# Output products of a fused convolution and SwiGLU kernel: the first group packed two quarters to a PSUM bank, with no filler products

## The chip, the cores and the metric

The kernel runs on one core of a Trainium2 chip. The metric is the device time of one launch in microseconds, the median of several runs. The kernel before takes 2728.72 us (three runs, 2728.63 to 2729.05).

## The reference, cut to what matters

```
# lightweight causal convolution: 7 taps per head, softmax over the taps
w = softmax(weight)                              # (8 heads, 7)
attn[b, s, h, :] = sum_k w[h, k] * x_pad[b, s + k, h, :]     # d_model 192
x = attn.reshape(32768, 192)

# RMS norm and SwiGLU, no bias
xn = x / sqrt(mean(x * x) + 1e-6) * rms_g
g, val = xn @ w_gate, xn @ w_val                 # (192, 1536) each
out = (silu(g) * val) @ w_out                    # (1536, 192), 32768 tokens
```

Everything is float32.

## The kernel before, in words

**Tiling.** The 32768 tokens are cut into 32 "pairs" of 1024 tokens; a pair is two groups (`g` = 0, 1) of 512 tokens. TensorE is used as two halves of 64 rows: the lower half (`h` = 0, partitions 0 to 63) and the upper half (`h` = 1). Each half runs a stream of its own products, and the two streams run beside each other. The eight PSUM banks of 128 x 512 float32 are split the same way: four for each half, handed out by two lists, `free[0]` and `free[1]`. A bank is taken from the head of the list when a product first needs one, and is appended when the last instruction that reads it has been emitted.

**Two stages for each pair.** In the first stage (`unit`, four times for each pair) the lower half computes the gate products and the upper half the value products. The contraction over 192 is three blocks of 64, and a unit covers three of the twelve blocks of 128 hidden columns. Instead of 18 products of 512 columns, each half does 15, on sums of the operands (`xc`, sums of tokens' blocks, and `wf`, sums of weights). Results are put together afterwards by ScalarE (A), VectorE (V) and GpSimd (G). All of it is in a written-out table, `PLAN`: each row has a time in ticks, a half, an engine and an action. `P` is a product, `F` copies a bank into another bank, onto which later products accumulate, `S` copies a bank to SBUF, `D` and `R` add a tile to a bank, `G` is the silu and `M` the product of gate and value. Products of a half stand 100 ticks apart; the upper half lags by `LAG` = 138 ticks; a unit starts every `SPAN` = 1509 ticks.

In the second stage (`outer`) the hidden tile `ht` (1536 x 1024 tokens) is multiplied by `w_out`. For each group `g` and each quarter `j` of 128 tokens there are twelve products (`f` = 0 to 11) of 192 columns in each half, 96 for a half and pair. The lower half contracts rows 0 to 63 of every block, the upper half rows 64 to 127. `low` copies the lower half's bank to `o_sb` (ScalarE), `upp` adds the upper half's bank (VectorE), and each then gives its bank back. `store` writes the group out. A product of this stage takes `STEP` = 37.5 ticks.

**What sets the order.** Everything is emitted from one heap, `line`, by planned tick, and within an engine instructions run in the order of emission; the ticks fix the order only, not the time. Engines wait for one another by semaphores, for instance a product that opens a bank waits for the last reader of that bank.

**Banks in the second stage.** For `g` = 0 the last unit's blocks (`f` = 9 to 11) are ready late, so all four quarters first do `f` = 0 to 8, each in a bank of its own (all four banks of the half), and then `f` = 9 to 11, each quarter followed by an evacuation of 192 columns. For `g` = 1 two quarters share a bank (columns 0 to 191 and 192 to 383) and are evacuated together, 384 columns at a time.

**The filler products.** [...] A bank that held two quarters has columns 384 to 511 unwritten, so the kernel issues an extra product of 128 columns into them (line 734) for the second shared bank of `g` = 1, which is the bank that the first `F` copy of the next pair takes:

```
            if g and j == 3 and f == 0:
                nc.tensor.matmul(
                    out=bank(h, bks[h])[:, 2 * D :],
                    ...
                    rhs=wo_sb[HALF[h], f, 0 : T - 2 * D], start=False, stop=True,
```

The condition holds once for each half and pair: 64 such products in all, each of which the profile shows as two passes.

**Other work beside.** The convolution of the pair after next (`conv`), its norm, its transposition through a DRAM scratch (`place`, `fetch`) and its operand sums (`x_sums`) are queued between these on ScalarE, VectorE and the DMA queue. In pair 0 the first stage is `plain` instead of `unit`: 18 plain products, emitted in the order of a string.

Lines that the steps use: the product of a unit is line 629, `F` and `S` on ScalarE are line 638 and on VectorE 640 and 642, `D` and `R` are line 651, the output product is line 723, the filler line 734, `low` line 743, `upp` line 747, `x_sums` line 565.

Of the kernel before, what the change touches and what calls it, by code (L numbers as in the profile page):

```python
# [19 lines left out]
def kernel(  # L20
# [10 lines left out]
    nc = tc.nc  # L31
    P = nc.NUM_PARTITIONS

    B, S, D = x.shape
# [8 lines left out]
    T = 512  # L43
# [7 lines left out]
    FC = DF // P  # L51
    NF = 3
# [129 lines left out]
    wo_sb = cst.tile([P, FC, D], F32, name="wo_sb")  # L182
# [28 lines left out]
    def load_out(i):  # L211
# [28 lines left out]
        out=taps[:], in0=w_sb[:], in1=stat[:].to_broadcast([P, H, K]), op=ALU.subtract  # L240
# [7 lines left out]
        out=taps[:], in0=taps[:], in1=ssum[:].to_broadcast([P, H, K]), op=ALU.mult  # L248
# [179 lines left out]
    HALF = (LOW, UPP)  # L428
# [116 lines left out]
    def x_op(i):  # L545
        return xb[:, i // KP, i % KP, :] if i < 2 * KP else xc[:, i - 2 * KP, :]
# [23 lines left out]
    free = [[0, 1, 2, 3], [0, 1, 2, 3]]  # L570

    def bank(half, i):
        return ps[half * 4 + i]


    whole = {(h, i) for h in range(2) for i in range(4)}


    line = []
# [2 lines left out]
    def put(at, do):  # L582
        heapq.heappush(line, (at, next(tick), do))
# [7 lines left out]
    def unit(u, base):  # L591


        ht = big.tile([P, 2, NF, T], F32, name="ht")
        bk, tl = {}, {}

        def hv(o):
            return ht[:, o // NF, o % NF, :]

        def new(v, h, product=False):  # L600
            bk[v, h] = free[h].pop(0)
            if product:
                whole.add((h, bk[v, h]))
            assert (h, bk[v, h]) in whole
            return bank(h, bk[v, h])[:]

        def old(v, h):
            return bank(h, bk[v, h])[:]

        def grab(k):  # L610
            tl[k] = tiles.pop(0)
            return tl[k][:]

        def tile_of(t, h):

            if (t, h) in tl:
                return tl[t, h][:]
            return hv(t[0]) if h else tl["g", t[0]][:]

        def plus(s):  # L620
            return ALU.add if s > 0 else ALU.subtract

        def do(h, eng, act, v, *rest):
            *rest, freed = rest
            e = {"V": nc.vector, "G": nc.gpsimd}.get(eng)
            if act == "P":
                i = rest[0]
                first = (v, h) not in bk
                nc.tensor.matmul(  # L629
                    out=new(v, h, True) if first else old(v, h), lhsT=wf[u][HALF[h], WAT[i], :],  # L630
                    rhs=x_op(XOP[i])[HALF[h]], start=first, stop=True, skip_group_check=True,
                )
            elif act in "FS":
                w, s = rest if act == "F" else (v, 1)
                src = old(w[0], h) if (w[0], h) in bk else tile_of(w, h)
                dst = new(v, h) if act == "F" else grab((v, h))
                if eng == "A":
                    nc.scalar.activation(out=dst, in_=src, func=AF.Copy, scale=float(s))  # L638
                elif s < 0:
                    e.tensor_scalar(out=dst, in0=src, scalar1=-1.0, scalar2=None, op0=ALU.mult)  # L640
                else:
                    e.tensor_copy(out=dst, in_=src)
            elif act == "C":
                a, b, s = rest
                a, b = tile_of(a, h), tile_of(b, h)
                e.tensor_tensor(out=grab((v, h)), in0=a, in1=b, op=plus(s))
            elif act in "DR":
                t, s = rest
                t, src = tile_of(t, h), old(v, h)
                dst = src if act == "D" else hv(v) if h else grab(("g", v))  # L650
                e.tensor_tensor(out=dst, in0=src, in1=t, op=plus(s))  # L651
            elif act == "G":
                src = tl["g", v][:] if v in results else old(v, 0)
                dst = src if v in results else grab(("g", v))
                nc.scalar.activation(out=dst, in_=src, func=AF.Silu)  # L655
            else:
                src = hv(v) if v in results else old(v, 1)
                e.tensor_tensor(out=hv(v), in0=src, in1=tl["g", v][:], op=ALU.mult)  # L658
            for k in freed:
                if k[0] == "b":  # L660
                    free[h].append(bk.pop((int(k[1]), h)))
                else:
                    tiles.append(tl.pop(("g", int(k[1])) if k[0] == "g" else (k, h)))

        for at, *a in PLAN:
            put(base + at, functools.partial(do, *a))
        return ht
# [48 lines left out]
    def outer(p, hts, base):  # L716


        def mm(h, bks, g, j, w, f, first, give=None):
            if first:  # L720
                bks[h] = free[h].pop(0)
                whole.discard((h, bks[h]))
            nc.tensor.matmul(  # L723
                out=bank(h, bks[h])[:, w : w + D],
                lhsT=hts[f // NF][HALF[h], g, f % NF, j * P : (j + 1) * P],
                rhs=wo_sb[HALF[h], f, :], start=(f == 0 and w == 0),
                stop=(f == FC - 1), skip_group_check=True,
            )

            if g and j == 3 and f == 0:
                nc.tensor.matmul(  # L734
                    out=bank(h, bks[h])[:, 2 * D :],
                    lhsT=hts[f // NF][HALF[h], g, f % NF, j * P : (j + 1) * P],
                    rhs=wo_sb[HALF[h], f, 0 : T - 2 * D], start=False, stop=True,
                    skip_group_check=True,
                )
                whole.add((h, bks[h]))  # L740

        def low(dst, bks, n):
            nc.scalar.copy(out=dst, in_=bank(0, bks[0])[:, 0:n])  # L743
            free[0].append(bks[0])

        def upp(dst, bks, n):
            nc.vector.tensor_tensor(out=dst, in0=bank(1, bks[1])[:, 0:n], in1=dst, op=ALU.add)  # L747
            free[1].append(bks[1])

        def store(g, o_sb):  # L750
            r = p * PT + g * T
            nc.sync.dma_start(
                out=out[r : r + T, :].rearrange("(j p) d -> p j d", p=P), in_=o_sb[:]
            )

        n = 0

        def mms(bks, g, j, w, fs, first):
            nonlocal n
            for i, f in enumerate(fs):  # L760
                for h in range(2):
                    at = base + n * STEP + h * LAG
                    put(at, functools.partial(mm, h, bks, g, j, w, f, first and i == 0))
                n += 1

        def evac(dst, bks, w):
            put(base + n * STEP + OVER, functools.partial(low, dst, bks, w))
            put(base + n * STEP + LAG + OVER, functools.partial(upp, dst, bks, w))

        for g in range(2):  # L770
            o_sb = outs.tile([P, T // P, D], F32, name="o_sb")
            if g == 0:

                bks = [{} for _ in range(4)]
                for j in range(4):
                    mms(bks[j], g, j, 0, range(0, FC - NF), True)
                for j in range(4):
                    mms(bks[j], g, j, 0, range(FC - NF, FC), False)
                    evac(o_sb[:, j, :], bks[j], D)
            else:  # L780
                for j in range(0, 4, 2):
                    b = {}
                    mms(b, g, j, 0, range(FC), True)
                    mms(b, g, j + 1, D, range(FC), False)
                    evac(o_sb[:, j : j + 2, :].rearrange("p j d -> p (j d)"), b, 2 * D)
            put(base + n * STEP + LAG + OVER + 1, functools.partial(store, g, o_sb))
# [33 lines left out]
    hts = []  # L820
    p, sl, v = plain(hts)
# [27 lines left out]
    for p in range(PAIRS):  # L849
        base = p * PAIR  # L850
        if p > 0:
            hts = []
            pl = place(p + 1)
            for u in range(NU):
                at = base + u * SPAN
# [51 lines left out]
```

## Time and profile before

| quantity | value |
|---|---|
| time, median of 3 | 2728.72 us |
| span of the profiled execution | 2724.8 us |
| PE busy | 2693.3 us, 99% of the span |
| VectorE, ScalarE, GpSimd busy | 84%, 81%, 46% |
| TensorE clock granted | 0.999 |
| one pair, from unit to unit (1304.28 to 1387.51) | 83.23 us |
| of it: four units | 51.81 us |
| of it: output products | 31.42 us |
| filler products in all (line 734) | 128 passes of 64x128 |

The profile counts a float32 product as two passes, each with its weight load (PEld) and its MATMUL. In a window of the timeline, the start of a MATMUL is when its turn in its half's stream came; the start of a weight load is usually the start of the MATMUL before it in the same half[...].

### The profile page before, as it was taken

What the parts mean: (1) busy time and instruction counts of PE and PEld (TensorE: products, weight loads), DVE (VectorE), ACT (ScalarE), POOL (GpSimd) and SP (SyncE); (2) the same over time, 40 slices, a digit from 0 to 9 for tenths busy, and PEclk for the clock granted to TensorE, in tenths of its full rate; (3) what the DMA queues carried; (4) which work ended last, traced back from release to release, by engine and by line L of the source; (5) the groups of instructions that cost most, each with busy time, mean ns of one, the idle gap of its engine ahead of it and who ended that gap; (6) DMA issues with size and microseconds to landing.
All of it is one profiled execution on the core that took longest, in us unless ns stands there. A gap on an engine that the chain in (4) does not pass through costs nothing.

```text
span 2724.8 us, 54269 instructions
## 1 busy us (share of the span) xinstructions
PE 2693.3 (99%) x20202; PEld 2071.0 (76%) x20202; DVE 2286.5 (84%) x3654; ACT 2212.3 (81%) x5026; POOL 1242.6 (46%) x1029
## 2 busy tenths in 40 slices
PE   6999999999999999999999999999999999999999
PEld 4767888777888778877777777778777777766777
DVE  8888888888889888888888888888898888888854
ACT  7788888888888888888888888888888888888854
POOL 3854344454344543444543445434445443454333
PEclk9999999999999999999999999999999999999999
DMA  5211222121222112121112221122211122211110
GB/s 145 82 42 44 67 57 68 42 52 54 56 68 62 41 45 67 57 68 43 51 54 56 68 62 42 45 67 57 68 44 52 52 56 68 62 42 44 48 36 13
DMA packets 94584, 152.90 MB, mean 56 GB/s; under 512 B 6768, under 2 KB 64880, under 8 KB 90232
## 3 DMA queue, kind: packets, MB, share of 16 engines
q1 hardware_dynamic: 93760, 149.41, 21.1%
q8 instruction: 158, 2.59, 0.4%
q14 instruction: 106, 0.87, 0.1%
q10 hardware_dynamic: 560, 0.03, 0.0%
HBM read 99.87 MB, written 49.55 MB: 55 GB/s over the span
## 4 chain that ended last, share of the span: by engine, by line
PE 96%; DVE 2%; DMA 1%; POOL 0%; ACT 0%; issue 0%; SPq 0%; DVEq 0%; POOLq 0%; ACTq 0%
PE ps L629 59%; PE ps L723 36%; PE ps L683 1%; DVE y L384 0%; DMA xb<-xd 0%; DMA x_sb<-in_x_dram 0%; POOL wf L321 0%; DVE xc L565 0%; PE ps L734 0%; DVE y L368 0%; ACT m L378 0%; DVE ht L700 0%; ACT xb L515 0%; DVE wf L291 0%; PE ps L495 0%
## 5 line engine op out<-in xcount | busy, mean ns | idle before, releaser
L629 PE MATMUL ps<-xc,wf 64*128 64x512 f32 x4960 | 1522.7, 593 | 2.6 <-DVE xc L565 2.6
L629 PEld LDWEIGHTS ps<-xc,wf 64*128 64x128 f32 x4960 | 771.2, 187 | 392.6 <-issue 209.8
L723 PE MATMUL ps<-wo_sb,ht 64*128 64x192 f32 x12288 | 1052.4, 323 | 2.0 <-DVE o_sb L747 1.8
L723 PEld LDWEIGHTS ps<-wo_sb,ht 64*128 64x128 f32 x12288 | 1047.7, 187 | 4.8 <-DVE o_sb L747 2.1
L629 PE MATMUL ps<-xb,wf 64*128 64x512 f32 x2480 | 1020.3, 589 | 0.0
L658 POOL TENSOR_TENSOR ht<-ht,tls 128x512 f32<-128x512 f32 x414 | 520.5, 1275 | 358.2 <-ACT tls L655 357.6
L638 ACT ACTIVATE tile<-ps 128x512 f32<-128x512 f32 x825 | 484.0, 596 | 139.9 <-PE ps L629 126.8
L629 PEld LDWEIGHTS ps<-xb,wf 64*128 64x128 f32 x2480 | 435.4, 187 | 199.0 <-issue 115.5
L378 ACT ACTIVATE m<-x_sb,taps 128x192 f32<-128x192 f32 x1520 | 543.4, 443 | 5.7 <-DMA x_sb<-in_x_dram 5.0
L384 DVE TENSOR_TENSOR y<-y,m 128x1536 f32<-128x1536 f32 x190 | 335.0, 1763 | 83.8 <-ACT m L378 78.8
L638 ACT ACTIVATE tls<-ps 128x512 f32<-128x512 f32 x663 | 376.0, 599 | 27.6 <-PE ps L629 16.1
L658 POOL TENSOR_TENSOR ht<-ht,tile 128x512 f32<-128x512 f32 x206 | 260.7, 1274 | 175.2 <-ACT tile L655 174.9
L401 POOL TENSOR_SCALAR r<-ss 128x8 f32<-128x8 f32 x31 | 27.2, 879 | 640.0 <-ACT sq L395 639.9
L655 ACT ACTIVATE tls<-tls 128x512 f32<-128x512 f32 x414 | 254.9, 625 | 16.5 <-DVE tls L651 15.0
L638 ACT ACTIVATE ps<-ps 128x512 f32<-128x512 f32 x372 | 216.3, 581 | 46.5 <-PE ps L629 35.7
L651 DVE TENSOR_TENSOR ht<-ps,tls 128x512 f32<-128x512 f32 x331 | 220.8, 681 | 0.0
L747 DVE TENSOR_TENSOR o_sb<-ps,o_sb 128x192 f32<-128x192 f32 (+1 forms) x192 | 77.5, 419 | 150.6 <-PE ps L629 107.8
L651 DVE TENSOR_TENSOR ht<-ps,tile 128x512 f32<-128x512 f32 x289 | 192.3, 681 | 0.0
L651 DVE TENSOR_TENSOR ps<-ps,tls 128x512 f32<-128x512 f32 x166 | 116.2, 700 | 87.8 <-PE ps L629 84.7
L651 DVE TENSOR_TENSOR tls<-ps,tile 128x512 f32<-128x512 f32 x248 | 166.9, 682 | 0.2 <-PE ps L629 0.2
L640 DVE TENSOR_SCALAR ps<-ps 128x512 f32<-128x512 f32 x248 | 164.1, 695 | 0.0
L743 ACT COPY o_sb<-ps 128x192 f32<-128x192 f32 (+1 forms) x192 | 70.3, 366 | 96.5 <-PE ps L723 96.5
(103 smaller groups left out, 2242.6 us busy)
## 6 DMA issues: line engine op xcount, KB each, us to landing
xb<-xd SPq DMA_DIRECT2D x124, 384.0 KB, 6.2
x_sb<-in_x_dram SPq DMA_DIRECT2D x24, 1344.0 KB, 5.8
out_dram<-o_sb SPq DMA_DIRECT2D x64, 384.0 KB, 2.6
xd<-nt SPq DMA_DIRECT2D x124, 192.0 KB, 3.4
x_sb<-in_x_dram SPq DMA_DIRECT2D x8, 1176.0 KB, 8.0
ht<-in_moe_w_gate_dram SPq DMA_DIRECT2D x12, 192.0 KB, 8.2
ht<-in_moe_w_val_dram SPq DMA_DIRECT2D x12, 192.0 KB, 6.4
tls<-in_moe_w_out_dram SPq DMA_DIRECT2D x8, 192.0 KB, 6.3
```

The source lines that it names most:

```text
L378: nc.scalar.mul(m[:, :, hs], xk[:, :, hs], taps[:, h, k : k + 1])
L384: nc.vector.tensor_tensor(out=y[:], in0=y[:], in1=m[:], op=ALU.add)
L629: nc.tensor.matmul(out=new(v, h, True) if first else old(v, h), lhsT=wf[u][HALF[h], WAT[i], :], rhs=x_op(XOP[i])[HALF[h]], start=first, st ...
L638: nc.scalar.activation(out=dst, in_=src, func=AF.Copy, scale=float(s))
L640: e.tensor_scalar(out=dst, in0=src, scalar1=-1.0, scalar2=None, op0=ALU.mult)
L651: e.tensor_tensor(out=dst, in0=src, in1=t, op=plus(s))
L655: nc.scalar.activation(out=dst, in_=src, func=AF.Silu)
L658: e.tensor_tensor(out=hv(v), in0=src, in1=tl["g", v][:], op=ALU.mult)
L683: nc.tensor.matmul(out=bank(h, bks[h])[:], lhsT=wf[u][HALF[h], k * NF + f, :], rhs=xb[HALF[h], g, k, :], start=(k == 0), stop=(k == KP - 1 ...
L723: nc.tensor.matmul(out=bank(h, bks[h])[:, w : w + D], lhsT=hts[f // NF][HALF[h], g, f % NF, j * P : (j + 1) * P], rhs=wo_sb[HALF[h], f, :] ...
L743: nc.scalar.copy(out=dst, in_=bank(0, bks[0])[:, 0:n])
L747: nc.vector.tensor_tensor(out=dst, in0=bank(1, bks[1])[:, 0:n], in1=dst, op=ALU.add)
```

## The change

The first group packs two quarters to a bank, as the second group did already. In `g` = 0, quarters 0 and 1 share one bank, quarters 2 and 3 another; they are evacuated 384 columns at a time, after the second quarter's last product. In `g` = 1, quarters 0 and 1 take the oldest free bank, and quarters 2 and 3 take one that has already been used so in this pair ("used"). So three banks of a half are partly written in a pair and the fourth stays whole. The filler products are gone. In the units, `pick` chooses by kind: an `F` copy takes the first free bank that is whole, a first product prefers one that is not, and makes it whole.

```diff
+    def pick(h, full):
+        i = next((i for i in free[h] if ((h, i) in whole) == full), free[h][0])
+        free[h].remove(i)
+        return i
...
         def new(v, h, product=False):
-            bk[v, h] = free[h].pop(0)
+            bk[v, h] = pick(h, not product)
...
         def mm(h, bks, g, j, w, f, first, give=None):
             if first:
-                bks[h] = free[h].pop(0)
+                bks[h] = free[h].pop(0) if first is True else pick(h, False)
                 whole.discard((h, bks[h]))
...
-            if g and j == 3 and f == 0:
-                nc.tensor.matmul(
-                    out=bank(h, bks[h])[:, 2 * D :],
-                    lhsT=hts[f // NF][HALF[h], g, f % NF, j * P : (j + 1) * P],
-                    rhs=wo_sb[HALF[h], f, 0 : T - 2 * D], start=False, stop=True,
-                    skip_group_check=True,
-                )
-                whole.add((h, bks[h]))
...
             if g == 0:
-                bks = [{} for _ in range(4)]
+                bks = [{}, {}]
                 for j in range(4):
-                    mms(bks[j], g, j, 0, range(0, FC - NF), True)
+                    mms(bks[j // 2], g, j, j % 2 * D, range(0, FC - NF), j % 2 == 0)
                 for j in range(4):
-                    mms(bks[j], g, j, 0, range(FC - NF, FC), False)
-                    evac(o_sb[:, j, :], bks[j], D)
+                    mms(bks[j // 2], g, j, j % 2 * D, range(FC - NF, FC), False)
+                    if j % 2:
+                        dst = o_sb[:, j - 1 : j + 1, :].rearrange("p j d -> p (j d)")
+                        evac(dst, bks[j // 2], 2 * D)
             else:
                 for j in range(0, 4, 2):
                     b = {}
-                    mms(b, g, j, 0, range(FC), True)
+                    mms(b, g, j, 0, range(FC), "used" if j else True)
                     mms(b, g, j + 1, D, range(FC), False)
```

More of the change, by code (lines that the diff above doesn't have):

```diff
@@ L762, in mms @@
                     at = base + n * STEP + h * LAG
-                    put(at, functools.partial(mm, h, bks, g, j, w, f, first and i == 0))
+                    put(at, functools.partial(mm, h, bks, g, j, w, f, first if i == 0 else False))
                 n += 1
```

## The prediction

> **What bounds the kernel now.** I read the page's busy times and groups first, then the chain of waits over two pairs, then the two stages of one pair, then single instructions around the places where the change moves a bank.
>
> ```profile
> PE 2693.3 (99%) x20202; PEld 2071.0 (76%) x20202; DVE 2286.5 (84%) x3654; ACT 2212.3 (81%) x5026; POOL 1242.6 (46%) x1029
> ...
> L734 PE MATMUL ps<-wo_sb,ht 64*128 64x128 f32 x128 | 24.4, 270 | 0.0
> ```
>
> ```profile
> 1305.65 50.75 PE ps L629 x235
> ...
> 1357.22 26.73 PE ps L723 x327
> 1383.95 0.03 PE ps L734
> 1383.98 1.22 PE ps L723 x14
> 1385.19 0.11 PE ps L734
> 1385.31 2.44 PE ps L723 x30
> ...
> 1388.88 50.75 PE ps L629 x235
> ```
>
> ```profile
> 1304.28:1356.08 51.81, 51.81 (x248) 32.30 (x247) 45.37 (x75) 44.72 (x83) 31.26 (x25) 1.00 0.09 24
> 1356.08:1387.51 31.42, 31.42 (x386) 31.42 (x384) 25.55 (x39) 24.72 (x76) 6.06 (x5) 1.00 0.40 108
> ```
>
> The second block is the chain of waits: between pairs it never leaves PE. The third is one pair's two stages (span, then PE, PEld, DVE, ACT, POOL): PE is busy in all of both. The pairs repeat every 83.23 us, so whatever shortens the PE stream of a pair by t, without a new wait, shortens the kernel by about 31 t (pair 0 is different, below).
>
> [...] passes of one half start 0.162, about 0.11 and 0.429 us apart. [...] here a load starts 0.43 us before the MATMUL that uses it in the 512-column stage. [...]
>
> **The change part by part.**
>
> *Removed: the filler.* It stands in both halves' streams, and the halves run beside each other, so it counts once for each pair:
>
> ```profile
> 1383.71 0.27 PE L734 MATMUL ps<-wo_sb,ht 64*128 64x128 f32 x1
> 1383.79 0.32 PE L723 MATMUL ps<-wo_sb,ht 64*128 64x192 f32 x1
> 1383.82 0.27 PE L734 MATMUL ps<-wo_sb,ht 64*128 64x128 f32 x1
> 1383.93 1.30 PE L723 MATMUL ps<-wo_sb,ht 64*128 64x192 f32 x13
> ```
>
> The lower half's two filler passes start at 1383.71 and 1383.82 and its next product at 1383.93: 2 x 0.11 = 0.22 us of stream. [...] The 24.4 us busy time of the row is an overstatement for the same reason. In pairs 1 to 31 this is 31 x 0.22 = 6.8 us. Pair 0 gives nothing: there PE waits at the end of the output stage for the next pair's operand sums (PE idle 2.6 us before the unit's products, "<-DVE xc L565"), which hang on the transfer xb<-xd, and no instruction of that chain is touched.
>
> *Fewer evacuations.* Four of 192 columns (352 ns on VectorE, 314 on ScalarE) become two of 384 (553 and 470): 0.3 us less for each engine and pair. Both engines are idle 12 to 14 us of a pair's 83.23 (70.92 and 69.43 busy), and the chain does not touch them. Worth nothing.
>
> *Banks inside the output stage.* Before, `g` = 1 opens a bank whose evacuation is planned 288 ticks (at 0.857 us for 100 ticks, 2.5 us) earlier; after the change it takes one freed over 1700 ticks earlier, in the unit. This removes the only wait of an output product for an evacuation, in pair 0: PE idle 1.8 us at 119.08, "<-DVE o_sb L747". Since PE then waits for the operand sums until 139.55 anyway, that time is only spent later: nothing.
>
> *Banks at the start of the next pair.* This is where a wait is added. Following the two free lists by hand, before the change the unit's first three products in each half take banks evacuated over 1000 ticks earlier, and the last-evacuated bank goes to the `F` copy, on the engine that evacuated it. After it, the copy takes the whole bank, free for some 3700 ticks, and the third product takes the bank of the last evacuation, planned 150 ticks earlier: lower half, tick 200, behind `low` at tick 50; upper half, tick 338, behind `upp` at tick 188. 150 ticks are 1.3 us, and evacuation (0.48 or 0.56) plus its own wait must fit. The instructions concerned, before the change:
>
> ```profile
> 1304.47 0.48 ACT L743 COPY o_sb<-ps 128x384 f32<-128x384 f32 x1 [1.39 <-PE ps L723]
> ...
> 1306.30 0.56 DVE L747 TENSOR_TENSOR o_sb<-ps,o_sb 128x384 f32<-128x384 f32 x1 [3.70 <-PE ps L629]
> ...
> 1305.57 0.19 PEld L629 LDWEIGHTS ps<-xb,wf 64*128 64x128 f32 x1
> 1306.78 0.19 PEld L629 LDWEIGHTS ps<-xb,wf 64*128 64x128 f32 x1 [0.17 <-issue]
> ```
>
> Lower half: `low` ends at 1304.95, and the weight load of the third product is at 1305.57. 0.6 us to spare: free. Upper half: `upp` ends at 1306.86, the load stood at 1306.78 and its MATMUL at 1307.21. The load is gated, 0.05 us after the release (below), so it moves to 1306.91, 0.13 later, still 0.30 ahead of its MATMUL. Behind it on PE are the other half's load (1306.85, for a MATMUL at 1307.28) and the upper half's next products. Does a load that comes 0.30 ahead cost time? The trace has two comparable places. In each unit a load gated by VectorE stands at 1398.48; the VectorE copy that releases it is the first of two that begin at 1397.74 and last 695 ns each, so it ended at 1398.43, and the MATMUL starts at 1398.74, just 0.43 after the half's last one: a lead of 0.26 costs nothing. And where the lead is only 0.03 (load at 1396.92, MATMUL at 1396.95) the MATMUL takes 666 ns rather than 589 and its half loses 77 ns. So the new wait costs nothing at a lead of 0.30; I take 0, with 77 ns a pair (2.4 us in all) as the upper bound of a short delay.
>
> ```profile
> 1398.48 0.18 PEld L629 LDWEIGHTS ps<-xb,wf 64*128 64x128 f32 x1
> ...
> 1397.74 1.32 DVE L640 TENSOR_SCALAR ps<-ps 128x512 f32<-128x512 f32 x2
> ...
> 1398.74 0.59 PE L629 MATMUL ps<-xb,wf 64*128 64x512 f32 x1
> ```
>
> `upp` stands at the same 2.03 us after the pair's first product in 29 of 30 pairs after pair 0; once (pair at 721.67) it is 0.35 later, which would cost about 0.15 us once. The remaining bank changes keep their distances (111 to 214 ticks in the units, as now).
>
> *Sum.* -6.8 + 0 + 0.15, so about -6.8 us: 2728.7 - 6.8 = 2721.9.
>
> **The rivals.**
> - *The new wait costs a little.* Each pair loses the 77 ns of a late load: 6.8 - 31 x 0.077 = 4.4 us gained, 2724.3. For: the margin is 0.04 us against the closest free case. Against: that case is free with less lead.
> - *The new wait becomes the bound, and the kernel is slower.* If `upp` fell behind one more VectorE instruction of 0.69 us, the load would come at 1307.60, the MATMUL, with the 0.11 us from a late load to its effective start, 0.50 late in every pair: 15.5 - 6.8, so 2737.4. For: VectorE is 85% busy and in order. Against: it is idle 3.5 us on average before this very `upp` (107.8 us in 31 times, by PE's release), so nothing queues ahead of it.
> - *Pair 0 gives its wait back as well.* 1.8 us more, 2720.1. For: the wait goes. Against: the operand sums end the same chain.
>
> **How the numbers follow.** The forecast has 0.78, the small cost 0.11, slower 0.07, pair 0 0.04. The range reaches from the pair 0 case, 2720.1, to just beyond the small cost, 2724.8. 0.2% is 5.5 us, so faster means under 2723.3: forecast and pair 0, 0.82. The small cost falls within 0.2%: 0.11. Slower by over 0.2%: 0.07.
>
> **What would show it.** Right: no line 734's passes, the output stage of a pair 31.20 us and the four units still 51.81, pairs every 83.01; the upper half's load 0.05 us after `upp` and its MATMUL still 2.93 us after the pair's first; PE idle before the first unit's products of pair 1 grown from 2.6 by about 2 us. Wrong: units that grow beyond 51.81 (the new wait), MATMULs of 666 ns at the third product, or pairs that stay at 83.23 though the filler is gone.

## The result, and the profile after

The changed kernel takes 2721.92 us, the median of six runs (2720.93 to 2723.08), against 2729.03 for the kernel before (2728.63 to 2732.65); the ratio is 0.9971, 95% interval 0.9958 to 0.9983. The forecast was 2721.9, faster.

The page of the changed kernel and two of its stages (span, then PE, PEld, DVE, ACT, POOL, PE clock); line 637 is now the unit's product, 731 the output product, 743 `upp`, 650 the copy that was 642:

```profile
PE 2687.9 (99%) x20074; PEld 2292.6 (84%) x20074; DVE 2288.5 (84%) x3590; ACT 2215.6 (81%) x4962; POOL 1243.0 (46%) x1029
```

```profile
1302.97:1354.77 51.80, 51.80 (x247) 42.27 (x246) 45.59 (x75) 45.16 (x83) 31.32 (x25) 1.00 0.10 24
1354.77:1385.97 31.20, 31.20 (x382) 31.20 (x380) 25.33 (x37) 24.50 (x74) 6.05 (x5) 1.00 0.42 109
```

There are 128 passes fewer (20202 - 20074). The units keep their 51.80 us, the output stage lost 0.22 (31.42 to 31.20), and pairs follow every 83.01 us rather than 83.23. PEld is busy longer in the units (42.27 us, before 32.30) with as many loads. That is no added work and costs nothing: the two halves' loads overlap less, since the halves now stand further apart (below). Two loads of 187 ns start 0.07 us apart before and take 0.26 us together; they start 0.21 apart after and take 0.40. The chain of waits, below, has only units and output products between two pairs; the filler's pieces are gone:

```profile
1304.04 51.06 PE ps L637 x236
...
1355.74 30.48 PE ps L731 x373
```

The place of the new wait, upper half, in the timeline of the changed kernel (the pair's first product starts at 1302.97):

```profile
1304.99 0.56 DVE L743 TENSOR_TENSOR o_sb<-ps,o_sb 128x384 f32<-128x384 f32 x1 [3.44 <-PE ps L637]
...
1305.60 0.34 PEld L637 LDWEIGHTS ps<-xb,wf 64*128 64x128 f32 x2
...
1305.76 0.59 PE L637 MATMUL ps<-xb,wf 64*128 64x512 f32 x1
1305.97 0.59 PE L637 MATMUL ps<-xc,wf 64*128 64x512 f32 x1
```

`upp` ends at 1305.55, the gated load follows 0.05 us later, and its MATMUL starts at 1305.76 with its usual 0.59 us. The wait is there and costs nothing. One thing differs from the forecast: the MATMUL starts 2.79 us after the pair's first product, not 2.93, so the load is only 0.15 us ahead, not 0.30. The upper half runs 0.21 us ahead of the lower half's next MATMUL (1305.97); before the change it was 0.07 (1307.21 and 1307.28).

At the start, in pair 0, the PE's wait for an evacuation is gone and the wait for the operand sums has grown, as foreseen. The groups by line (busy time, mean, and last the idle time before them) of the kernel before, then of the changed one:

```profile
L629 PE MATMUL ps<-xc,wf 64*128 64x512 f32 x4960 | 1522.7, 593 | 2.6 <-DVE xc L565 2.6
L723 PE MATMUL ps<-wo_sb,ht 64*128 64x192 f32 x12288 | 1052.4, 323 | 2.0 <-DVE o_sb L747 1.8 <-POOL wo_sb L283 0.3
```

```profile
L637 PE MATMUL ps<-xc,wf 64*128 64x512 f32 x4960 | 1496.3, 594 | 4.9 <-DVE xc L565 4.9
L731 PE MATMUL ps<-wo_sb,ht 64*128 64x192 f32 x12288 | 1040.6, 323 | 0.3 <-POOL wo_sb L283 0.3
```

The idle time before the units' products grew from 2.6 us to 4.9. But the four units of pair 1 (the pair after that wait) take 55.69 us instead of 54.02, at a granted clock of 0.94 instead of 1.00. This was not foreseen, and the third experiment is about it.

### The profile page after: what moved, and what is told of

The parts are those of the page before. It is cut to its first block, busy times and chain, and to the rows that moved or that the text cites. A ratio compares the mean times of both kernels' runs of the same rounds, so it can differ in the third digit from the quotient of the medians.

```text
span 2719.7 us, 53761 instructions
## 1 busy us (share of the span) xinstructions
PE 2687.9 (99%) x20074; PEld 2292.6 (84%) x20074; DVE 2288.5 (84%) x3590; ACT 2215.6 (81%) x4962; POOL 1243.0 (46%) x1029
## 4 chain that ended last, share of the span: by engine, by line
PE 96%; DVE 2%; DMA 1%; POOL 0%; ACT 0%; issue 0%; SPq 0%; DVEq 0%; POOLq 0%; ACTq 0%
PE ps L637 59%; PE ps L731 36%; PE ps L691 1%; DVE y L384 0%; DMA xb<-xd 0%; PE ps L495 0%; DMA x_sb<-in_x_dram 0%; ACT m L378 0%; POOL wf L321 0%; DVE xc L565 0%; DVE ht L708 0%; DVE y L368 0%; DVE wf L291 0%; DMA xd<-nt 0%; POOL wo_sb L283 0%
## 5 line engine op out<-in xcount | busy, mean ns | idle before, releaser
L637 PE MATMUL ps<-xc,wf 64*128 64x512 f32 x4960 | 1496.3, 594 | 4.9 <-DVE xc L565 4.9
L637 PEld LDWEIGHTS ps<-xc,wf 64*128 64x128 f32 x4960 | 828.7, 187 | 266.2 <-issue 94.2
L731 PE MATMUL ps<-wo_sb,ht 64*128 64x192 f32 x12288 | 1040.6, 323 | 0.3 <-POOL wo_sb L283 0.3
L731 PEld LDWEIGHTS ps<-wo_sb,ht 64*128 64x128 f32 x12288 | 1035.8, 187 | 2.5 <-POOL wo_sb L283 0.6
L637 PE MATMUL ps<-xb,wf 64*128 64x512 f32 x2480 | 992.0, 589 | 0.0
L378 ACT ACTIVATE m<-x_sb,taps 128x192 f32<-128x192 f32 x1520 | 537.3, 446 | 5.4 <-DMA x_sb<-in_x_dram 4.6
L637 PEld LDWEIGHTS ps<-xb,wf 64*128 64x128 f32 x2480 | 456.6, 187 | 100.7 <-issue 35.8
L743 DVE TENSOR_TENSOR o_sb<-ps,o_sb 128x384 f32<-128x384 f32 x128 | 70.8, 554 | 156.1 <-PE ps L637 100.6
L395 ACT ACTIVATE sq<-y 128x192 f32<-128x192 f32 x248 | 90.3, 364 | 64.2 <-DVE y L384 58.3
```

What stands on the lines that cost most here:

```text
L378: nc.scalar.mul(m[:, :, hs], xk[:, :, hs], taps[:, h, k : k + 1])
L395: nc.scalar.activation(out=sq[:], in_=y[:, j, :], func=AF.Square, accum_out=ss[:, j : j + 1])
L637: nc.tensor.matmul(out=new(v, h, True) if first else old(v, h), lhsT=wf[u][HALF[h], WAT[i], :], rhs=x_op(XOP[i])[HALF[h]], start=first, st ...
L731: nc.tensor.matmul(out=bank(h, bks[h])[:, w : w + D], lhsT=hts[f // NF][HALF[h], g, f % NF, j * P : (j + 1) * P], rhs=wo_sb[HALF[h], f, :] ...
```

## The experiments

### Is the filler the whole gain?

The kernel before, without line 734's products and otherwise the same:

```diff
             if g and j == 3 and f == 0:
-                nc.tensor.matmul(
-                    out=bank(h, bks[h])[:, 2 * D :],
...
-                )
                 whole.add((h, bks[h]))
```

> The kernel before with line 734's filler products left out and nothing else changed: banks, evacuations and their order stay as before. It leaves out the accumulation in columns 384 to 511 of the bank of each pair's first F copies [...]. Theory (the filler is the whole gain, the rest of the change is worth nothing): output stage 31.20 us, units 51.81, pairs every 83.01, 2722 us as the changed kernel. Rival (the packing or the looser banks bring part of the gain): pairs between 83.01 and 83.23, time between 2722 and 2729. In pair 0 the PE wait for an evacuation (1.8 us) stays, and the wait before the first unit stays at about 2.6 us.

Measured: 2721.68 us (2721.37 to 2723.32), ratio 0.9975 (0.9965 to 0.9984). Units and output stage of one pair:

```profile
1303.07:1354.87 51.80, 51.80 (x248) 32.30 (x247) 45.36 (x75) 44.71 (x83) 31.25 (x25) 1.00 0.10 24
1354.87:1386.07 31.20, 31.20 (x382) 31.20 (x380) 25.55 (x39) 24.72 (x76) 6.06 (x5) 1.00 0.41 109
```

The same 51.80 and 31.20 as the changed kernel, with the old banks and evacuations (DVE 39 and ACT 76 instructions in the second stage, as before the change). In pair 0 the 1.8 us wait stays. The PE wait for the sums is 1.8 us, not about 2.6. Without these products the output's relative error is 0.48, so what is added onto `F`'s copies needs a bank that products have written in all 512 columns (`whole` lists such banks). By what mechanism is not shown.

The changed kernel, with the filler put back where it was:

```diff
+            if g and j == 3 and f == 0:
+                nc.tensor.matmul(
+                    out=bank(h, bks[h])[:, 2 * D :],
...
```

> The changed kernel with the two filler products of each pair put back at their old place; packing, evacuations and bank order stay changed. Theory: pairs every 83.23 us again, output stage 31.42, units 51.81, time 2729 within 2 us of the kernel before: packing and the new wait are worth nothing in the steady pairs. Rival (the new wait costs, the packing gives): something other than 83.23.

Measured: 2730.88 us (2727.66 to 2732.47), ratio 1.0005 (0.9998 to 1.0011).

```profile
1307.14:1358.94 51.80, 51.80 (x247) 42.44 (x246) 45.60 (x75) 45.11 (x83) 31.26 (x25) 1.00 0.10 24
1358.94:1390.37 31.43, 31.43 (x387) 31.42 (x385) 25.33 (x37) 24.48 (x74) 6.05 (x5) 1.00 0.41 108
```

31.43 again, and pairs every 83.23. In the steady pairs the filler is the whole difference in both directions; packing, fewer evacuations and the new wait add nothing. What the packing does is let the filler go. Its median is 1.85 us above that of the kernel before, within the noise (the interval includes 1). It is about the size of what pair 1 loses here too: its units take 55.73 us at a granted clock of 0.94. With the filler alone left out they keep 54.02 us at 1.00, so that loss comes with the new packing and its banks, not with the filler's absence.

### How near is the new wait?

If the last `upp` of a pair ended later, when would it cost? The first way is to cut it into pieces (4, then 8, then 12), each release coming with the last piece:

```diff
-        def upp(dst, bks, n):
-            nc.vector.tensor_tensor(out=dst, in0=bank(1, bks[1])[:, 0:n], in1=dst, op=ALU.add)
+        def upp(dst, bks, n, parts=1):
+            for i in range(parts):
+                s = slice(i * n // parts, (i + 1) * n // parts)
+                nc.vector.tensor_tensor(
+                    out=dst[:, s], in0=bank(1, bks[1])[:, s], in1=dst[:, s], op=ALU.add
+                )
...
+            parts = 4 if last else 1
```

> The changed kernel, with the last upp of each pair as four additions of 96 columns instead of one of 384, to make the new wait later by a little. Estimate: four of them take about 0.85 us rather than 0.56, so the bank is released 2.88 us after the pair's first product, the upper half's load stands at 2.93 with its MATMUL due at 2.93. Theory (a load may come up to about 0.11 us before its MATMUL without cost): the MATMUL is about 0.1 us late, pairs every 83.1, time 2725. Rival (a late load costs nothing, streams absorb it): 83.01, 2722. Rival (any gated load costs 77 ns or more): the changed kernel itself would have shown it, and here it would be 0.2 or more.

> The changed kernel with the last upp of each pair as eight additions of 48 columns. With the step from piece to piece at about 0.12 us the bank would be released about 3.0 us after the pair's first product and the upper half's load stand at 3.05, past the 2.79 at which its MATMUL starts in the changed kernel. Theory from the run with four pieces (the upper half's stream is pushed back once and keeps its new distance to the lower half, so the wait is paid once): pairs still every 83.01, the MATMUL later by the same amount in every pair, 2722 to 2724. Rival (the prediction's way of costing, each pair pays what the load is late): 0.25 us or more for each pair, 2730 or more.

> The same with twelve additions of 32 columns. Release about 3.3 us after the pair's first product, the upper half's load at about 3.35. The lower half's next product, queued behind that load, starts at 3.43. Theory (the upper half can slip freely until the lower half's next load is held up too): near the edge, pairs between 83.01 and 83.15, 2722 to 2727. Rival (each pair pays the lateness): 0.6 us for each pair, 2740.

The second way is to put it behind another VectorE instruction (the group's `store` moves back with it):

```diff
-            put(base + n * STEP + LAG + OVER, functools.partial(upp, dst, bks, w))
+            late = 137 if last and p < PAIRS - 1 else 0
+            put(base + n * STEP + LAG + OVER + late, functools.partial(upp, dst, bks, w))
```

> The changed kernel with the last upp of each pair planned 137 ticks later, at tick 325 of the next pair, so that it stands behind the VectorE copy of line 650 (S of block 5, planned at 322) and just ahead of the product that needs its bank (338). The copy ends 3.46 us after the pair's first product, so upp would end at 4.0 and the load come at 4.07, its MATMUL 1.2 us late. Theory (the new wait is a real dependency with about 0.2 us to spare): each pair longer by 0.6 to 1.2 us, the lower half's stream being held behind it too, so 2741 to 2759 us. Rival (the order of the queue doesn't matter because the halves can drift apart): 2722 to 2726.

Measured, all after the pair's first product, in a pair in the middle of each trace:

| last `upp` | load at | MATMUL at, took | units | pairs every | time |
|---|---|---|---|---|---|
| one piece (changed kernel) | 2.63 us | 2.79, 589 ns | 51.80 | 83.01 | 2721.9 us |
| four pieces | 2.83 | 2.94, 589 ns | 51.81 | 83.01 | 2723.7 (2721.2 to 2725.4) |
| eight pieces | 3.09 | 3.09, 693 ns | 51.92 | 83.12 | 2728.5 (2727.4 to 2730.6) |
| twelve pieces | 3.35 | 3.35, 693 ns | 52.17 | 83.38 | 2736.2 (2735.7 to 2737.0) |
| behind the copy | 3.98 | 3.98, 694 ns | 52.80 | 84.01 | 2754.8 (2753.6 to 2755.6) |

With four pieces the estimate of the release was a little high (2.78 us, not 2.88; the four take 0.75 us, not 0.85) and the steady pairs pay nothing, against the 0.1 us that was expected. Its time lies within the range of the changed kernel when that ran again (2721.51 to 2724.41, below). In pair 2 the timeline shows the price paid once (pair's first product at 225.44), and in a later pair not again (first product at 1304.55):

```profile
228.28 0.69 PE L637 MATMUL ps<-xb,wf 64*128 64x512 f32 x1
...
1307.49 0.59 PE L637 MATMUL ps<-xb,wf 64*128 64x512 f32 x1
```

The first starts at 2.84 with its load and takes 0.69; the later one starts at 2.94, 0.11 behind its load, and takes 0.59. The upper half has slipped by 0.1 us against the lower half and stays there; since both halves have the same work, the period doesn't change. With eight pieces the slip has an end. The loads of both halves queue behind the gated one (PEld of the run with eight pieces, then PE; first product at 1307.82):

```profile
1310.91 0.18 PEld L637 LDWEIGHTS ps<-xb,wf 64*128 64x128 f32 x1 [0.33 <-DVE o_sb L745]
1310.92 0.18 PEld L637 LDWEIGHTS ps<-xc,wf 64*128 64x128 f32 x1
```

```profile
1310.91 0.69 PE L637 MATMUL ps<-xb,wf 64*128 64x512 f32 x1
```

Here, with twelve pieces and behind the copy, the upper half's MATMUL before it starts at 2.66, so this one is due at 2.66 + 0.43 = 3.09: the half has slipped to 3.09 and no further. From there each pair pays. The three costs, 0.11, 0.37 and 1.00 us (83.12, 83.38, 84.01 less 83.01), are the load's time less 2.98 (3.09, 3.35, 3.98), and 2.98 is the latest due time, 3.09, less the 0.11 us by which a load must lead. For eight and twelve pieces both written expectations missed, one by taking the slip as unbounded, the other by charging each pair for all of it. Behind the copy the wait costs what was expected. The pieces also keep VectorE busy longer (0.75 us for four and 1.01 for eight, against 0.56 in one), but behind the copy `upp` is one piece again, and the cost lies on the same line, so it goes with the load's time. That 3.09 is the limit is measured in three kernels; what sets it wasn't tried. The trace with eight pieces shows only where the lower half pays: not behind the gated load, where its MATMUL at 3.43 is on time with 589 ns, but at 11.24 us after the pair's first product. A load of its own that waits for VectorE comes there 0.01 us ahead, and the MATMUL takes 682 ns.

### The idle time in pair 0

PE in the changed kernel at the start of pair 1:

```profile
136.99 1.19 PE L637 MATMUL ps<-xc,wf 64*128 64x512 f32 x1 [4.04 <-DVE xc L565]
...
141.70 1.06 PE L637 MATMUL ps<-xb,wf 64*128 64x512 f32 x1
```

and busy times, clock (the number before the DMA share) and transfers of the kernel before, then of the changed one, from 116 to 128 us and from 136 to 144 us (for the kernel before, with the four units of pair 1):

```profile
116.00:128.00 12.00, 10.21 (x102) 9.91 (x102) 7.41 (x8) 8.70 (x30) 11.01 (x13) 0.86 0.79 176
...
136.00:144.00 8.00, 5.55 (x29) 3.58 (x31) 7.20 (x15) 3.37 (x8) 1.55 (x2) 1.00 0.17 51
136.68:190.70 54.02, 52.24 (x244) 33.82 (x246) 49.08 (x84) 44.41 (x82) 31.29 (x25) 1.00 0.09 23
```

```profile
116.00:128.00 12.00, 12.00 (x152) 12.00 (x150) 8.51 (x8) 9.97 (x33) 11.37 (x13) 1.00 0.65 151
...
136.00:144.00 8.00, 6.18 (x19) 4.11 (x21) 5.67 (x13) 1.78 (x3) 0.00 (x0) 0.57 0.06 18
```

Before, PE idled 1.8 us at 117; the granted clock was still 1.00 until 120 and then 0.55, 0.50 and 0.50 in the three microseconds to 123, with MATMULs of up to 524 ns where 322 is usual, in an output stage that had to wait for the operand sums anyway. After, it idles 4.0 us at 133, and the slow stretch falls on the first products of pair 1, where nothing hides it: the clock is 0.50 from 136.99 to 143, with MATMULs of 1.06 us where 0.59 is usual. How long PE has to idle for this, the traces do not show. In the kernel before, the gap of 1.8 us at 117 was followed by the lowered clock (0.86 over the 12 us), while another of 1.8 us, which ended at 139.55, was not (1.00). In the second trace of the changed kernel, from the repetition at the end of this section, a gap of 3.35 us was followed by a MATMUL of 0.67 us, and only after the next gap, 1.78 us, did one take 1.19. With the filler back and with four pieces, too, the slowest MATMUL of the units takes 1.19 us; in the kernel before and with the filler alone left out it takes 693 ns. To test whether the idle time is the cause, PE is kept busy there with four extra products:

```diff
+        if p == 0:
+            def warm():
+                for _ in range(4):
+                    nc.tensor.matmul(
+                        out=ps[7][:], lhsT=wf[0][:, 0, :],
+                        rhs=wo_sb[:].rearrange("p f d -> p (f d)")[:, 0:T],
+                        start=True, stop=True, skip_group_check=True,
+                    )
+            put(base + OUT - 1, warm)
```

> The changed kernel with four extra full products of 512 columns (into the free bank of the upper half, on weights that are there) queued on PE in pair 0, just ahead of the first product of pair 1, where PE idles 4.0 us and the MATMULs after it take twice as long. Theory (the idle time is what lowers PE's speed at the start of pair 1): the MATMULs there take 589 ns instead of 1060 to 1190, the units of pair 1 take 54.0 us instead of 55.7, and the time is about 1.6 us shorter, 2720. Rival (the slow stretch comes anyway, at a fixed time after the start): same slow MATMULs around 137 to 143 us, 2722. Rival (the extra products hold PE up): pair 1 starts later, 2723 or more.

The stage of four units of pair 1 in the changed kernel, and then in this one:

```profile
136.99:192.68 55.69, 54.86 (x244) 37.49 (x246) 49.16 (x84) 44.62 (x82) 31.25 (x25) 0.94 0.09 22
```

```profile
139.11:193.14 54.02, 52.24 (x244) 33.92 (x246) 49.12 (x84) 44.39 (x82) 31.24 (x25) 1.00 0.09 23
```

54.02 us at full clock, 1.67 less, and the slowest MATMUL of the units takes 693 ns, so the slow stretch doesn't come anyway. But in this run pair 1 starts 2.1 us later (139.11; its output stage of pair 0 already began 1.7 us later), and the time, 2721.22 us (2718.84 to 2722.80), doesn't stand clear of the changed kernel's. So both kernels ran once more on one chip:

> The changed kernel as it is, beside the next one on the same chip. 2722 us, units of pair 1 at 55.7 us with a granted clock of about 0.94 in them, pairs every 83.01.

> The changed kernel with the four extra products in pair 0 once more. If the 1.66 us that the units of pair 1 gained with them reaches the end, its median is 1.2 to 2 us under that of the changed kernel in this call (2720.3); if what comes before pair 1 varies as much from run to run, the two ranges overlap and the medians differ by under 1 us.

Measured: the changed kernel 2723.25 us (2721.51 to 2724.41, eleven runs), with the extra products 2721.30 (2720.80 to 2722.13, eight runs). The medians lie 1.95 us apart, as expected of the first case, though the ranges still overlap. In the traces the units of pair 1 take 56.74 us at a granted clock of 0.94 in the changed kernel, 1 us more than was expected of it, and 53.74 at 1.00 with the extra products; pair 1 starts at 138.47 and 139.03, the output stage of pair 0 at 102.69 and 103.08. Against the kernel before the ratios are 0.9978 (0.9970 to 0.9987) and 0.9972 (0.9961 to 0.9982). With the extra products the kernel is the faster of the two, by little.

## Why the prediction was right

- *The filler, 31 x 0.22 = 6.8 us.* Right in each pair: 83.23 to 83.01, the output stage 31.42 to 31.20. Taking it out alone and putting it back alone show that it is the whole effect in steady pairs. That it counts once, though both halves issue it, and at its spacing in the stream (0.11 us a pass), not at its recorded 270 ns, is what made this term right. The trace before shows the spacings that the prediction names: passes of one half start 0.162 us apart at 192 columns, 0.11 at 128 and 0.429 at 512. It also shows why the row's 24.4 us is too much: the filler's two records of 270 ns start 0.11 us apart, so they overlap.
- *Fewer evacuations, looser banks in the output stage: nothing.* Right: units and output stage are as long with them as without.
- *The new wait: nothing.* Right in size, and the load does come 0.05 us after `upp`. The reasoning was wrong in one part: it took the upper half's due time as fixed at 2.93 us after the pair's first product. The two halves' distance is free within a range (2.79 in the changed kernel, 2.94 with four pieces, up to 3.09). The rule for a late load, 0.11 us ahead or its MATMUL pays, held wherever it was read (leads of 0, 0.01, 0.03 and 0.08 us cost 104, 93, 77 and 28 ns, lead and loss adding up to about 0.11 us each time; the last, with twelve pieces, is the lower half's MATMUL at 3.43). The real spare time is up to 2.98 - 2.63 = 0.35 us, more than the 0.2 that the prediction implies.
- *The slower rival* (`upp` behind a VectorE instruction of 0.69 us) is real as a mechanism. Brought about in an experiment, it made the load 1.35 us later, and each pair paid 1.00 us. Its own size, 0.50 us a pair for a load 3.32 us after the first product, was too high: by the measured limit it is 3.32 - 2.98 = 0.34. It did not happen by itself: VectorE was idle 3.70 us before `upp` in the trace before and 3.44 in the trace after.
- *The sum.* It names 0.15 us for one late pair and then drops it; added up, it is 6.65 us and 2722.1. In the changed kernel's trace no pair after pair 1 took other than 83.01 us.
- *Pair 0: nothing.* The step that was off: it put at nothing what a longer idle stretch does to the clock. The wait moved, as foreseen, from the evacuation to the operand sums, but the slow stretch behind it moved with it, from hidden to exposed (clock 0.50 from 121 to 123 us before, from 136.99 to 143 after): the units of pair 1 take 1.7 us more. In the two profiled executions the span therefore fell by 5.1 us (2724.8 to 2719.7) and not by 6.8. The medians of this comparison fell by 7.1, those of the later one on another chip by 5.6 (2728.89 to 2723.25). The term that was missing and the noise cancelled, so the hit to a tenth of a microsecond is luck; runs of the same kernel differ by 2 to 5 us, and in its two traces the changed kernel starts pair 1 at 136.99 and at 138.47.

## What to carry to other kernels

Where the stream of one engine is the bound, price an instruction by its spacing in the stream, and multiply by the repetitions in which nothing else hides it. A new wait is judged by how far ahead the waiting instruction stood of the one that needs it, so look for a gated case in the same trace that was free and one that was not. Time saved in front of a later wait is not simply lost: here gaps of 1.79, 0.81 and 1.78 us became one of 4.04 and one of 0.83, and PE came out of the long one at a lowered clock (0.57 from 136 to 144 us).

## What the runs showed of the hardware that was not expected

- The two row halves of PE, which run equal streams here, kept a distance that history set: 0.21 us in the changed kernel, 0.07 in the one before and with four pieces. A single delay of one half (0.1 us with four pieces) was never made up and cost nothing afterwards, up to a limit here of 3.09 us after the pair's first product; beyond it the pair paid, one for one with the load's time.
- A weight load that leads its 512-column MATMUL by 0.11 us was free. One that starts with it made the MATMUL 693 ns long instead of 589. In between, lead and loss added up to 0.11 us.
- In the kernel before, one gap of 1.8 us in PE's work was followed by a lowered clock (0.50 from 121 to 123 us) and a later one was not (1.00 from 139.5 to 141). Four full products, 3.70 us of PE time, queued where PE had idled 4.04 us brought the next stage from 55.69 us at a granted clock of 0.94 to 54.02 at 1.00.
